# Sigmoid attention and a routed feed-forward block on one core: a third PSUM buffer for the scores, two single banks shared by everything else, and the input loads cut and ordered anew

## The chip, the cores and the metric

The kernel runs on one core of one Trainium2 chip. The metric is the device time of one execution in microseconds (us), lower is better. A core has five engines that run side by side: TensorE (PE in the profile, with its weight loads as PEld), VectorE (DVE), ScalarE (ACT), GpSimd (POOL) and SyncE (SP), which here only issues DMA transfers. PSUM, the memory that TensorE writes its results to, has 8 banks of 512 fp32 columns for each partition.

## What is computed

Everything is fp32. Attention with a sigmoid in place of the softmax runs over 8 sequences, 12 heads, 448 tokens and head size 64. Then, for each sequence, the 128 tokens with the highest gate score pass through a two-layer feed-forward block, and the result is added to their rows.

```python
scores = scale * np.matmul(q, k.transpose(0, 1, 3, 2)) - np.log(S)
attn = 1.0 / (1.0 + np.exp(-scores))
x = np.matmul(attn, v)            # (B,H,S,D) -> (B,S,H*D) = (8,448,768)
scores = np.einsum('bsd,d->bs', x, w_gate)
out = x.copy()
for b in range(B):
    top_idx = np.argpartition(-scores[b], capacity)[:capacity]     # capacity 128
    xe = x[b, top_idx]
    ye = np.maximum(xe @ w1, 0.0) @ w2                             # 768 -> 1024 -> 768
    g = 1.0 / (1.0 + np.exp(-scores[b, top_idx]))
    out[b, top_idx] = x[b, top_idx] + g[:, None] * ye
```

## The kernel before

The attention is cut into 24 **items** of four heads (two pairs), three items to a sequence. The order on every engine is the order in which `stream` writes the program out (L378 to L396).

For item `i`, `load` (L71) brings k, q and the item's part of v, 16 DMAs on SP, two items ahead. The two raw buffers of k and q are free again once `turn` has read them. Every DMA of SP also waits for the one issued eight before it, so at most eight are under way. `turn` (L155) turns k and q over on VectorE, one item ahead. `scores` (L169) makes the scores in seven steps, `n` = 0 to 6: a pair of matmuls into one two-bank PSUM buffer `psc`, then one sigmoid on ScalarE (L185) that reads it into `attnT`. Steps 0 to 2 are the first pair of heads, 3 to 5 the second, 6 the last 64 tokens of both. `psc` has two buffers, so step `n` waits for the sigmoid of step `n - 2`. `values` (L188) multiplies by v into two banks `pav`: first the last 64 tokens (L194, from `raw_h`), then the full blocks (L200, from `raw_v`); VectorE copies each bank out to `xT` (L205).

An item stands in `stream` as: steps 0 to 3, `fill(2i)`, steps 4 to 6, `turn(i+1)`, `fill(2i+1)`, `values(i)`. `fill(s)` (L366) writes what two tables hold for **slot** `s`:

- `back` (L212): slots `2i+2` and `2i+3`. TensorE transposes one pair of heads of item `i` into the single bank `ps1` (L219); VectorE copies it into `x_b` (L221), the sequence's rows. There is one `x_b`.
- `store_and_gate` (L226), `rank` (L244), `select` (L269), `turn_rows` (L288) of sequence `b`, at slots 6b+7, +9, +11 and +12: the rows go out by two 1.3 MB stores on SP (to the output and to a scratch copy `x_d`, L228 and L230), the gate is computed on VectorE, the tokens are ranked (L247 to L265), the chosen rows are gathered by POOL from `x_d` (L283) and transposed. All their PSUM results are in `ps1`.
- `ffn1` (L298) and `ffn2` (L311), slots 6b+13 to 6b+18, in the single bank `psf`: four slots with two of the eight 128-column blocks of the hidden layer each, with a relu on ScalarE after four blocks (L309); then two slots with 384 output columns each, closed by VectorE (L324). `scatter` (L328) writes the rows back to the output. A later sequence's stores wait for it on SP.

So there are 2 x 2 banks for `psc`, 2 for `pav`, 1 for `ps1` and 1 for `psf`: all 8. Slots 48 and up stand behind the last item (the **tail**). `load_weights` (L148) issues both weight matrices (3 MB each) as two DMAs on POOL's queue; in POOL's own order nothing holds them, so they start at the very beginning.

Of the kernel before, what the change touches and what calls it, by code (L numbers as in the profile page):

```python
# [16 lines left out]
def kernel(  # L17
# [51 lines left out]
    raws = {}  # L69

    def load(i):  # L71
        b, g = divmod(i, NQ)
# [1 line left out]
        tiles = []
        for nm, src in (("k", k), ("q", q)):

            t = raw.tile([P, 2, TB * Dh], F32, name=f"raw_{nm}")
            for j in range(2):
                for e in range(2):
                    p0 = (2 * j + e) * TT  # L80
                    nc.sync.dma_start(
                        out=t[p0:p0 + TT, :, 0:RUN],
                        in_=bass.AP(
                            tensor=src.tensor,
                            offset=src.offset + (b * H + h0 + j) * S * Dh + e * TT,
                            ap=[[TB * Dh, TT], [2 * S * Dh, 2], [1, RUN]]),
                    )
            tiles.append(t)

        tv = vals.tile([P, 4, NF * Dh], F32, name="raw_v")  # L90
        for m in range(4):
            nc.sync.dma_start(
                out=tv[m * TT:(m + 1) * TT],
                in_=bass.AP(tensor=v.tensor,
                            offset=v.offset + (b * H + h0) * S * Dh + NF * m * Dh,
                            ap=[[TB * Dh, TT], [S * Dh, 4], [1, NF * Dh]]))

        th = vals.tile([P, 2, Dh], F32, name="raw_h")
        for pr in range(2):
            for m in range(2):  # L100
                p0 = (2 * pr + m) * TT
                nc.sync.dma_start(
                    out=th[p0:p0 + TT],
                    in_=bass.AP(tensor=v.tensor,
                                offset=(v.offset + (b * H + h0 + 2 * pr) * S * Dh
                                        + (4 * NF + m) * Dh),
                                ap=[[TB * Dh, TT], [S * Dh, 2], [1, Dh]]))
# [47 lines left out]
    def turn(i):  # L155
# [3 lines left out]
        src = raws[i][0].rearrange("p a (r d) -> p a r d", d=Dh)
        for pr in range(2):  # L160
            nc.vector.transpose(  # L161
                kT[i][:, pr, :4 * NF],
                src[:, pr, :4 * NF, 0:TT].rearrange("p (m c) d -> p c m d", c=NF))
        nc.vector.transpose(kT[i][:, :, 4 * NF:], src[:, :, 4 * NF:, 0:TT])
        qT[i] = head.tile([P, 2, TB, TT], F32, name="qT")
        src = raws[i][1].rearrange("p a (r d) -> p a r d", d=Dh)
        nc.vector.transpose(qT[i], src[:, :, :, 0:TT])  # L167
# [20 lines left out]
    def values(i):  # L188
        tv, th = raws[i][2:]
        out_t = [ps_o.tile([P, S], F32, name="pav") for _ in range(2)]  # L190
        for pr in range(2):
            for j in range(2):
                p = slice(pr * Dh, (pr + 1) * Dh)
                nc.tensor.matmul(out_t[pr][j * Dh:(j + 1) * Dh], th[p, j, :],  # L194
                                 attn[i][p, 2 * NF, j, :], start=True, stop=False)
        xT[i] = head.tile([P, 2, S], F32, name="xT")
        for pr in range(2):
            for c in range(NF):
                for j in range(2):
                    nc.tensor.matmul(  # L200
                        out_t[pr][j * Dh:(j + 1) * Dh],
                        tv[:, 2 * pr + j, c * Dh:(c + 1) * Dh],
                        attn[i][:, pr * NF + c, j, :],
                        start=False, stop=(c == NF - 1))
            nc.vector.tensor_copy(  # L205
                xT[i][:, pr].rearrange("p (t r) -> p r t", r=TB),
                out_t[pr].rearrange("p (r t) -> p r t", t=TT))
        del raws[i], qT[i], kT[i], attn[i]
# [220 lines left out]
```

## Time and profile before

| | |
|---|---|
| runs | median 584.09 us of 3 (583.95 to 584.29) |
| the profiled execution | 583.43 us, of which the span of the profile is 581.7 us |
| TensorE busy | 514.4 us, 88% of the span |
| VectorE, ScalarE, POOL busy | 235.8 us (41%), 174.0 us (30%), 31.3 us (5%) |
| the 16 DMA engines | 88.93 MB moved; share busy 0.8 to 0.9 in the first quarter of the span, mostly 0.2 to 0.7 in the rest |

"Busy" counts a matmul's record from its start to its modelled end. Matmuls are pipelined, so records overlap, and a stretch can read as busy although TensorE begins nothing in it. What a wait costs is read from the distance between the starts of two instructions instead. Each fp32 matmul has two records, so "x8" in a row of the trace is four matmuls; the listings of the program's order further down count matmuls.

### The profile page before, as it was taken

The numbers are of one execution on the slowest core, as the hardware profiler recorded it, in microseconds if no ns is written. First come the engines' busy times: TensorE is split into PE (matmuls) and PEld (weight loads), VectorE is DVE, ScalarE is ACT, GpSimd is POOL, SyncE is SP. The second block draws the span as 40 slices with busy tenths as digits, with TensorE's granted clock in tenths as the row PEclk, the third lists the DMA queues.
The fourth block names the chain that finished last, engine by engine and source line by source line (L and its number), as shares of the span: only waits on it lengthen the run. The fifth ranks groups of instructions, "written<-read, shape, count | busy, mean of one in ns | idle before, by whom it ended". The sixth has DMA issues, their size and how long they took to land.

```text
span 581.7 us, 7332 instructions
## 1 busy us (share of the span) xinstructions
PE 514.4 (88%) x2896; PEld 271.3 (47%) x2896; DVE 235.8 (41%) x481; ACT 174.0 (30%) x193; POOL 31.3 (5%) x43
## 2 busy tenths in 40 slices
PE   0819996889999999999999999999999999998995
PEld 0203332334554455545554455545544554558582
DVE  0013353635372356426371356326371456137100
ACT  0404444233522332522522422522532422400000
POOL 5000000000000000001000000001000000000100
PEclk9978999898999999999999999999999999999998
DMA  8999999893976188724976198724875150006000
GB/s 199 333 230 205 208 197 274 191 216 107 237 160 149 44 264 194 167 70 149 221 159 147 59 266 191 163 60 169 215 160 132 59 191 1 0 28 219 27 28 27
DMA packets 46995, 88.93 MB, mean 153 GB/s; under 512 B 12848, under 2 KB 25136, under 8 KB 46960
## 3 DMA queue, kind: packets, MB, share of 16 engines
q1 hardware_dynamic: 44288, 75.52, 53.0%
q0 software_dynamic: 2672, 12.93, 7.0%
q8 instruction: 23, 0.38, 0.3%
q14 instruction: 12, 0.10, 0.1%
HBM read 63.26 MB, written 25.17 MB: 152 GB/s over the span
## 4 chain that ended last, share of the span: by engine, by line
PE 71%; DMA 9%; ACT 8%; issue 6%; DVE 4%; SPq 0%; POOLq 0%; POOL 0%; ACTq 0%; DVEq 0%
PE psc L180 19%; PE pav L200 18%; PE psf L320 12%; PE psf L306 11%; ACT attnT L185 8%; DMA raw_q<-in_q_dram 5%; PE ps L219 4%; PE pav L194 4%; DMA raw_h<-in_v_dram 2%; DMA x_d<-x_b 2%; DVE junk L234 1%; PE ps L247 1%; PE ps L274 1%; DVE junk L259 1%; PE ps L294 1%
## 5 line engine op out<-in xcount | busy, mean ns | idle before, releaser
L185 ACT ACTIVATE attnT<-psc,bias_s 128x896 f32<-128x896 f32 x168 | 161.7, 1005 | 287.3 <-PE psc L180 287.2
L180 PE MATMUL psc<-qT,kT 64*128 64x448 f32 (+1 forms) x768 | 160.0, 584 | 46.2 <-DVE qT L167 28.7
L180 PEld LDWEIGHTS psc<-qT,kT 64*128 64x128 f32 (+1 forms) x768 | 54.5, 178 | 137.9 <-ACT attnT L185 70.8
L200 PE MATMUL pav<-attnT,raw_v 128*64 128x448 f32 x576 | 113.7, 544 | 0.0
L306 PE MATMUL psf<-xeT,w_sb 128*128 128x128 f32 x768 | 92.2, 276 | 1.7 <-DVE oe L324 1.0
L320 PE MATMUL psf<-w_sb,hT 128*128 128x384 f32 x256 | 90.8, 497 | 1.9 <-DVE oe L324 1.2
L306 PEld LDWEIGHTS psf<-xeT,w_sb 128*128 128x128 f32 x768 | 88.4, 192 | 2.8 <-DVE oe L324 1.8
L221 DVE COPY x_b<-ps 112x512 f32<-112x512 f32 x48 | 33.1, 689 | 135.1 <-PE ps L219 122.0
L200 PEld LDWEIGHTS pav<-attnT,raw_v 128*64 128x64 f32 x576 | 39.3, 137 | 73.5 <-issue 70.7
L205 DVE COPY xT<-pav 128x448 f32<-128x448 f32 x48 | 43.0, 922 | 52.9 <-PE pav L200 52.9
L320 PEld LDWEIGHTS psf<-w_sb,hT 128*128 128x128 f32 x256 | 46.7, 194 | 28.4 <-DVE oe L324 2.1
L161 DVE STREAM_TRANSPOSE kT<-raw_k 128x384 f32<-128x384 f32 x48 | 24.7, 552 | 29.2 <-DMA raw_k<-in_k_dram 29.2
L219 PEld LDWEIGHTS ps<-iden,xT 128*112 128x112 f32 x192 | 19.8, 134 | 35.6 <-issue 25.8
L219 PE MATMUL ps<-iden,xT 128*112 128x128 f32 x192 | 31.5, 287 | 3.2 <-DVE x_b L221 3.2
L309 ACT ACTIVATE hT<-psf 128x512 f32<-128x512 f32 x16 | 9.6, 597 | 78.5 <-PE psf L306 78.5
L234 DVE CUSTOM_DVE_ANT_0 junk<-x_b,wg_b 112x768 f32<-112x768 f32 x32 | 30.7, 958 | 1.8
L324 DVE SCALAR_TENSOR_TENSOR oe<-psf,gate,xe 128x384 f32<-128x384 f32 x16 | 9.9, 617 | 52.4 <-PE psf L320 30.2
L167 DVE STREAM_TRANSPOSE qT<-raw_q 128x896 f32<-128x896 f32 x24 | 25.8, 1075 | 10.5 <-DMA raw_h<-in_v_dram 6.4
L194 PE MATMUL pav<-attnT,raw_h 64*64 64x448 f32 x192 | 24.9, 578 | 2.8 <-ACT attnT L185 2.8
L259 DVE SCALAR_TENSOR_TENSOR junk<-rep,earlier 112x448 f32<-112x448 f32 x32 | 21.9, 685 | 1.4
L259 DVE SCALAR_TENSOR_TENSOR junk<-rep,ones_row 112x448 f32<-112x448 f32 x32 | 21.9, 685 | 1.2
L283 POOL DMA_INDIRECT xe<-x_d,row x8 | 8.0, 1006 | 266.8 <-DVE idx L279 229.5
(38 smaller groups left out, 117.6 us busy)
## 6 DMA issues: line engine op xcount, KB each, us to landing
raw_k<-in_k_dram SPq DMA_DIRECT2D x96, 216.0 KB, 4.8
raw_q<-in_q_dram SPq DMA_DIRECT2D x96, 216.0 KB, 6.8
out_dram<-x_b SPq DMA_DIRECT2D x8, 1344.0 KB, 6.5
x_d<-x_b SPq DMA_DIRECT2D x8, 1344.0 KB, 11.4
raw_v<-in_v_dram SPq DMA_DIRECT2D x96, 96.0 KB, 4.3
w_sb<-in_moe_w_dram POOLq DMA_DIRECT2D x2, 3072.0 KB, 25.9
raw_h<-in_v_dram SPq DMA_DIRECT2D x96, 16.0 KB, 2.4
wg_b<-in_moe_w_gate_dram POOLq DMA_DIRECT2D x1, 336.0 KB, 8.2
```

The costliest lines, as they stand in the source:

```text
L167: nc.vector.transpose(qT[i], src[:, :, :, 0:TT])
L180: nc.tensor.matmul(psc[p0:p0 + np_, j, :S], kT[i][d, pr, rows, :].rearrange("e r t -> e (r t)"), qT[i][d, pr].rearrange("e r t -> e (r t)" ...
L185: nc.scalar.activation(attn[i][:, n], psc[:, :, :S], AF.Sigmoid, bias=bias_s, scale=QK_SCALE)
L194: nc.tensor.matmul(out_t[pr][j * Dh:(j + 1) * Dh], th[p, j, :], attn[i][p, 2 * NF, j, :], start=True, stop=False)
L200: nc.tensor.matmul(out_t[pr][j * Dh:(j + 1) * Dh], tv[:, 2 * pr + j, c * Dh:(c + 1) * Dh], attn[i][:, pr * NF + c, j, :], start=False, sto ...
L205: nc.vector.tensor_copy(xT[i][:, pr].rearrange("p (t r) -> p r t", r=TB), out_t[pr].rearrange("p (r t) -> p r t", t=TT))
L219: nc.tensor.transpose(ps[:CP, c, :], xT[i][:, pr, c * CP:(c + 1) * CP], iden)
L221: nc.vector.tensor_copy(x_tiles[b][:, :, hp * P:(hp + 1) * P], ps[:CP])
L234: nc.vector.tensor_tensor_reduce(out=junk, in0=x_b[:, c, :], in1=wg_b, scale=1.0, scalar=0.0, op0=ALU.mult, op1=ALU.add, accum_out=tg[:, c ...
L259: nc.vector.scalar_tensor_tensor(out=junk, in0=rep[:, :S], scalar=rep[:, S + c:S + c + 1], in1=mask, op0=cmp, op1=ALU.mult, accum_out=cnt[ ...
L306: nc.tensor.matmul(ps[:, f % 4, :n], w1_sb[:, t, f * P:(f + 1) * P], xeT[:, t, :n], start=(t == 0), stop=(t == KD - 1))
L320: nc.tensor.matmul(ps[:n, :ND], hT[:, t, :n], w2_sb[:, t, cols], start=(t == 0), stop=(t == KF - 1))
```

## The change

Banks: `psc` gets a third two-bank buffer (6 banks). The other two banks are the single buffers `oa` and `ob`. `oa` takes the first half of `values`, `back`, `rank`, `select` and `turn_rows`; `ob` takes the second half of `values`, `ffn1` and `ffn2`.

Order within `values`: the full blocks of the first pair, the last 64 tokens of both, the full blocks of the second pair. Each half is copied out as before.

Feed-forward: `ffn1` takes three slots (blocks 3, 3, 2, a relu after each), `ffn2` three slots with 256 columns each. The six slots stay the same.

Loads: item 0's k and q come by pair (8 + 8 small DMAs), and `turn(0)` works by pair. v comes per sequence, all 12 heads in 8 DMAs, into two buffers; its last 64 tokens are loaded to both halves of the partitions, twice the bytes of before for that part. Sequence 0's v comes in two parts around item 1's load; later ones are issued at item `3b+1`. The weights are cut in 14 pieces on SP, two at each item 1 to 7, behind that item's loads.

```diff
-    ND = D // 2
+    ND = D // 3
-    vals = ctx.enter_context(tc.tile_pool(name="vals", bufs=3))
+    vals = ctx.enter_context(tc.tile_pool(name="vals", bufs=2))
-    ps_sc = ctx.enter_context(tc.tile_pool(name="ps_sc", bufs=2, space=PSUM))
-    ps_o = ctx.enter_context(tc.tile_pool(name="ps_o", bufs=2, space=PSUM))
-    ps_f = ctx.enter_context(tc.tile_pool(name="ps_f", bufs=1, space=PSUM))
-    ps_1 = ctx.enter_context(tc.tile_pool(name="ps_1", bufs=1, space=PSUM))
+    ps_sc = ctx.enter_context(tc.tile_pool(name="ps_sc", bufs=3, space=PSUM))
+    ps_a = ctx.enter_context(tc.tile_pool(name="ps_a", bufs=1, space=PSUM))
+    ps_b = ctx.enter_context(tc.tile_pool(name="ps_b", bufs=1, space=PSUM))
...
+    def load_v(b, h0=0, h1=H):
+        if h0 == 0:
+            raw_v[b] = (vals.tile([P, H, NF * Dh], F32, name="raw_v"),
+                        vals.tile([P, H, Dh], F32, name="raw_h"))
+        tv, th = raw_v[b]
...
+        for m in range(4):
+            nc.sync.dma_start(out=tv[m * TT:(m + 1) * TT, h0:h1], in_=rows(NF * m, NF))
+        for m in range(4):
+            nc.sync.dma_start(out=th[m * TT:(m + 1) * TT, h0:h1],
+                              in_=rows(4 * NF + m % 2, 1))
 
-    load(0)
+    load(0, (slice(0, 1), slice(1, 2)))
+    load_v(0, 0, 4)
     load(1)
+    load_v(0, 4, H)
...
-    def load_weights():
-        for w, src in ((w1_sb, moe_w1), (w2_sb, moe_w2)):
-            nc.gpsimd.dma_start(out=w, in_=src.rearrange("(t p) f -> p t f", p=P))
+    def load_weights(i):
+        for n in (2 * i - 2, 2 * i - 1):
+            if 0 <= n < KD:
+                nc.sync.dma_start(out=w1_sb[:, n], in_=moe_w1[n * P:(n + 1) * P, :])
+            elif KD <= n < KD + KF:
+                n -= KD
+                nc.sync.dma_start(out=w2_sb[:, n], in_=moe_w2[n * P:(n + 1) * P, :])
...
     def values(i):
...
+        out_t = [ps_a.tile([P, 512], F32, name="oa"), ps_b.tile([P, 512], F32, name="ob")]
...
+        full(0, True, False)
         for pr in range(2):
             for j in range(2):
                 p = slice(pr * Dh, (pr + 1) * Dh)
...
+                nc.tensor.matmul(out_t[pr][j * Dh:(j + 1) * Dh, :S],
+                                 th[p, 4 * g + 2 * pr + j, :],
+                                 attn[i][p, 2 * NF, j, :], start=(pr == 1), stop=(pr == 0))
+        out(0)
+        full(1, False, True)
+        out(1)
...
-            for f in range(KF):
-                put(long, s + 2 + f // 2, ffn1, b, n, f)
-            s += 2 + KF // 2
-            for part in range(2):
+            s += 2
+            for f0 in range(0, KF, 3):
+                f1 = min(f0 + 3, KF)
+                for f in range(f0, f1):
+                    put(long, s, ffn1, b, n, f0, f1, f)
+                s += 1
+            for part in range(D // ND):
                 for t0 in range(0, KF, 2):
-                    put(long, s + part, ffn2, b, n, part, t0)
-            put(long, s + 1, scatter, b, n)
-            s += 2
+                    put(long, s, ffn2, b, n, part, t0)
+                s += 1
+            put(long, s - 1, scatter, b, n)
...
-        turn(0)
+        turn(0, (slice(0, 1), slice(1, 2)))
         late_consts()
         for i in range(NI):
             if i + 2 < NI:
                 load(i + 2)
-            if i == 1:
-                load_weights()
+            if i % NQ == 1 and i // NQ + 1 < B:
+                load_v(i // NQ + 1)
+            load_weights(i)
```

Three places show how this moves instructions. The first is SP's queue from the start of the program to the load of item 2. Before (the number behind a tile's name tells its buffers apart):

```order
L81 DMA raw_k_87<-in_k_dram 32x2x864 x4
L81 DMA raw_q_92<-in_q_dram 32x2x864 x4
L92 DMA raw_v_97<-in_v_dram 32x4x192 x4
L102 DMA raw_h_102<-in_v_dram 32x2x64 x4
L81 DMA raw_k_107<-in_k_dram 32x2x864 x4
L81 DMA raw_q_112<-in_q_dram 32x2x864 x4
L92 DMA raw_v_117<-in_v_dram 32x4x192 x4
L102 DMA raw_h_122<-in_v_dram 32x2x64 x4
L81 DMA raw_k_170<-in_k_dram 32x2x864 x4
L81 DMA raw_q_175<-in_q_dram 32x2x864 x4
```

The same queue in the change, up to the first two weight pieces (`raw_k_84` and `raw_q_85` are item 0's):

```order
L82 DMA raw_q_85<-in_q_dram 32x864 x4
L105 DMA raw_v_102<-in_v_dram 32x4x192 x4
L107 DMA raw_h_103<-in_v_dram 32x4x64 x4
L82 DMA raw_k_112<-in_k_dram 32x2x864 x4
L82 DMA raw_q_113<-in_q_dram 32x2x864 x4
L105 DMA raw_v_102<-in_v_dram 32x8x192 x4
L107 DMA raw_h_103<-in_v_dram 32x8x64 x4
L82 DMA raw_k_175<-in_k_dram 32x2x864 x4
...
L105 DMA raw_v_253<-in_v_dram 32x12x192 x4
L107 DMA raw_h_254<-in_v_dram 32x12x64 x4
L154 DMA w1_sb_137<-in_moe_w1_dram 128x1024 x2
```

The load of item 2 (`raw_k_175`) now stands behind the whole of sequence 0's v, and the weights stand in this queue, behind the loads, instead of in POOL's.

The second place is TensorE from the second half of an item, through `values`, to the next item's first half. Before:

```order
L306 MATMUL psf<-xeT,w_sb 128x128 x12
L194 MATMUL pav<-attnT,raw_h 64x448 x4
L200 MATMUL pav<-attnT,raw_v 64x448 x12
L180 MATMUL psc<-qT,kT 128x448 x8
L219 MATMUL ps_2571<-iden,xT 112x128 x4
```

In the change:

```order
L324 MATMUL ob<-xeT,w_sb 128x128 x18
L205 MATMUL oa<-attnT,raw_v 64x448 x6
L220 MATMUL oa<-attnT,raw_h 64x448 x2
L220 MATMUL ob<-attnT,raw_h 64x448 x2
L205 MATMUL ob<-attnT,raw_v 64x448 x6
L188 MATMUL psc<-qT,kT 128x448 x8
L237 MATMUL oa<-iden,xT 112x128 x4
```

The value matmuls now write the banks that the feed-forward block (`ob`) and the transposes of `back` (`oa`) have just used and will use next, and the last 64 tokens stand in their middle.

The third place is TensorE in the tail, from the last `back` on. Before:

```order
L219 MATMUL ps_3200<-iden,xT 112x128 x4
L306 MATMUL psf<-xeT,w_sb 128x128 x24
L247 MATMUL ps_3246<-diag,ones 112x448
L249 MATMUL ps_3246<-tok_gate_142,iden 112x4
L306 MATMUL psf<-xeT,w_sb 128x128 x24
L274 MATMUL ps_3301<-tok_gate_142,sel 128x2 x4
L320 MATMUL psf<-w_sb,hT 128x384 x8
```

In the change:

```order
L237 MATMUL oa<-iden,xT 112x128 x4
L324 MATMUL ob<-xeT,w_sb 128x128 x36
L265 MATMUL oa<-diag,ones 112x448
L267 MATMUL oa<-tok_gate_145,iden 112x4
L324 MATMUL ob<-xeT,w_sb 128x128 x12
L338 MATMUL ob<-w_sb,hT 128x256 x8
L292 MATMUL oa<-tok_gate_145,sel 128x2 x4
```

The last sequence's `rank` (L247, now L265) stands behind 36 matmuls of the sequence before it instead of 24, and its `select` behind one more group of eight.

## Rows read from the trace of the kernel before

**Rows 1.** Timeline of the start: start us, length us, engine, line, what [idle before, releaser].

```profile
44.07 5.81 PE L180 MATMUL psc<-qT,kT 64*128 64x448 f32 x16 [13.09 <-DVE qT L167]
...
74.84 1.77 PE L180 MATMUL psc<-qT,kT 64*128 64x448 f32 x8
...
89.37 1.77 PE L180 MATMUL psc<-qT,kT 64*128 64x448 f32 x8
...
99.59 0.69 DVE L221 COPY x_b<-ps 112x512 f32<-112x512 f32 x1 [9.18 <-DMA x_d<-x_b]
...
139.16 2.84 PE L306 MATMUL psf<-xeT,w_sb 128*128 128x128 f32 x24
```

**Rows 2.** Waits over the whole span: engine line <- releaser: us, times, longest.

```profile
PEld psc L180 <- ACT attnT L185: 70.8, 79, 1.3
...
DVE x_b L221 <- DMA x_d<-x_b: 13.1, 2, 9.2
```

**Rows 3.** Timeline of one item in the middle: TensorE, ScalarE, one copy of VectorE.

```profile
206.95 0.98 PE L194 MATMUL pav<-attnT,raw_h 64*64 64x448 f32 x8
207.86 4.73 PE L200 MATMUL pav<-attnT,raw_v 128*64 128x448 f32 x24
212.52 1.77 PE L180 MATMUL psc<-qT,kT 64*128 64x448 f32 x8
213.65 1.91 ACT L185 ACTIVATE attnT<-psc,bias_s 128x896 f32<-128x896 f32 x2 [8.82 <-PE psc L180]
214.71 1.92 PE L180 MATMUL psc<-qT,kT 64*128 64x448 f32 x8 [0.42 <-ACT attnT L185]
216.56 0.65 PE L219 MATMUL ps<-iden,xT 128*112 128x128 f32 x4
...
217.25 0.69 DVE L221 COPY x_b<-ps 112x512 f32<-112x512 f32 x1 [3.69 <-PE ps L219]
...
219.82 1.77 PE L180 MATMUL psc<-qT,kT 64*128 64x448 f32 x8
221.95 0.98 PE L180 MATMUL psc<-qT,kT 64*64 64x448 f32 x8 [0.35 <-ACT attnT L185]
222.87 0.65 PE L219 MATMUL ps<-iden,xT 128*112 128x128 f32 x4
```

**Rows 4.** Page part 6, DMA issues: how many, KB each, median us to landing.

```profile
raw_k<-in_k_dram SPq DMA_DIRECT2D x96, 216.0 KB, 4.8
...
x_d<-x_b SPq DMA_DIRECT2D x8, 1344.0 KB, 11.4
raw_v<-in_v_dram SPq DMA_DIRECT2D x96, 96.0 KB, 4.3
w_sb<-in_moe_w_dram POOLq DMA_DIRECT2D x2, 3072.0 KB, 25.9
raw_h<-in_v_dram SPq DMA_DIRECT2D x96, 16.0 KB, 2.4
```

**Rows 5.** Windows: last three columns are PEclk, DMA share, GB/s.

```profile
2.00:14.00 12.00, 0.00 (x0) 0.00 (x0) 1.23 (x3) 0.24 (x1) 6.70 (x14) 1.00 1.00 223
14.00:38.00 24.00, 13.74 (x64) 4.64 (x64) 2.34 (x4) 6.76 (x7) 0.00 (x0) 0.95 1.03 314
```

**Rows 6.** Windows of 1 us around TensorE's first long stop; same columns.

```profile
36.00:37.00 1.00, 0.00 (x0) 0.00 (x0) 0.39 (x2) 0.00 (x0) 0.00 (x0) 0.50 1.07 301
...
49.00:50.00 1.00, 1.00 (x6) 0.27 (x5) 0.00 (x0) 1.00 (x2) 0.00 (x0) 0.91 1.05 211
```

**Rows 7.** Timeline of the tail, TensorE.

```profile
515.27 0.65 PE L219 MATMUL ps<-iden,xT 128*112 128x128 f32 x4
...
544.33 0.49 PE L294 MATMUL ps<-iden,xe 128*128 128x128 f32 x3
...
558.10 5.62 PE L306 MATMUL psf<-xeT,w_sb 128*128 128x128 f32 x48 [0.75 <-ACT hT L309]
...
570.61 5.43 PE L320 MATMUL psf<-w_sb,hT 128*128 128x384 f32 x16 [0.77 <-DVE oe L324]
```

More of the change, by code (lines that the diff above doesn't have):

```diff
@@ L72, in load @@
+    ps_b = ctx.enter_context(tc.tile_pool(name="ps_b", bufs=1, space=PSUM))
+    raws, raw_v = {}, {}
+    def load(i, prs=(slice(0, 2),)):
         b, g = divmod(i, NQ)
         h0 = 4 * g
[L74 to L78, printed above, removed]
+        raws[i] = [raw.tile([P, 2, TB * Dh], F32, name=f"raw_{nm}") for nm in "kq"]
+        for pr in prs:
+            for t, src in zip(raws[i], (k, q)):
@@ L79, in load @@
                 for e in range(2):
[L80 to L90, printed above, removed]
@@ L91, in load @@
-        for m in range(4):
[L92 to L107, printed above, removed]
@@ L108, in load @@
-        raws[i] = tiles + [tv, th]
-    load(0)
+                    for j in range(2):
+                        p0 = (2 * j + e) * TT
+                        nc.sync.dma_start(
+                            out=t[p0:p0 + TT, pr, 0:RUN],
+                            in_=bass.AP(
+                                tensor=src.tensor,
+                                offset=(src.offset + e * TT
+                                        + (b * H + h0 + j + 2 * pr.start) * S * Dh),
+                                ap=[[TB * Dh, TT], [2 * S * Dh, pr.stop - pr.start],
+                                    [1, RUN]]))
@@ L146, in late_consts, with turn @@
                 fill=1.0, base=-c * CP, pattern=[[1, S]], channel_multiplier=-1)
[L148 to L150 removed]
+    def load_weights(i):
[5 more added lines that the diff above has]
+                nc.sync.dma_start(out=w2_sb[:, n], in_=moe_w2[n * P:(n + 1) * P, :])
     qT, kT, attn, pav, xT = {}, {}, {}, {}, {}
[L155 removed]
+    def turn(i, prs=(slice(0, 2),)):
         kT[i] = head.tile([P, 2, TB, TT], F32, name="kT")
[L159 to L164, printed above, removed]
[L165 to L167 removed]
+        qT[i] = head.tile([P, 2, TB, TT], F32, name="qT")
+        sk, sq = [t.rearrange("p a (r d) -> p a r d", d=Dh) for t in raws[i]]
+        for a in prs:
+            for pr in range(a.start, a.stop):
+                nc.vector.transpose(
+                    kT[i][:, pr, :4 * NF],
+                    sk[:, pr, :4 * NF, 0:TT].rearrange("p (m c) d -> p c m d", c=NF))
+            nc.vector.transpose(qT[i][:, a], sq[:, a, :, 0:TT])
+            nc.vector.transpose(kT[i][:, a, 4 * NF:], sk[:, a, 4 * NF:, 0:TT])
+        del raws[i]
     def scores(i, n):
@@ L188, in values, with full, out @@
     def values(i):
-        tv, th = raws[i][2:]
-        out_t = [ps_o.tile([P, S], F32, name="pav") for _ in range(2)]
+        b, g = divmod(i, NQ)
+        tv, th = raw_v[b]
+        out_t = [ps_a.tile([P, 512], F32, name="oa"), ps_b.tile([P, 512], F32, name="ob")]
+        xT[i] = head.tile([P, 2, S], F32, name="xT")
+        def full(pr, start, stop):
+            for c in range(NF):
+                for j in range(2):
+                    nc.tensor.matmul(
+                        out_t[pr][j * Dh:(j + 1) * Dh, :S],
+                        tv[:, 4 * g + 2 * pr + j, c * Dh:(c + 1) * Dh],
+                        attn[i][:, pr * NF + c, j, :],
+                        start=start and c == 0, stop=stop and c == NF - 1)
+        def out(pr):
+            nc.vector.tensor_copy(
+                xT[i][:, pr].rearrange("p (t r) -> p r t", r=TB),
+                out_t[pr][:, :S].rearrange("p (r t) -> p r t", t=TT))
+        full(0, True, False)
         for pr in range(2):
@@ L193, in values @@
                 p = slice(pr * Dh, (pr + 1) * Dh)
[L194 to L208, printed above, removed]
+                nc.tensor.matmul(out_t[pr][j * Dh:(j + 1) * Dh, :S],
[4 more added lines that the diff above has]
+        out(1)
+        del qT[i], kT[i], attn[i]
     x_tiles = {}
```

32 lines of the change are left out of this document (17 added, 15 removed).

## The prediction

> **What bounds the kernel now.** I read the page first: TensorE is busy for 88% of the span, no other engine for more than 41%. That does not say that only fewer matmuls can help, because a record that overlaps the next one hides a late start. So I went to the waits [rows 2]: TensorE's weight loads for the scores wait 70.8 us for sigmoids, in 79 waits of at most 1.3 us. Then to the timeline of one item in the middle of the run [rows 3], which shows what such a wait costs, and to the start and the tail [rows 1, 7], where TensorE really stands still. The kernel has three parts. In the **start**, up to 139.2 us [rows 1], the DMA queues are full and TensorE waits for them. In the **middle**, up to 515.3 us, TensorE sets the pace. In the **tail**, the last 66.4 us [rows 7], a chain through ranking, gather and the last feed-forward block does.
>
> **The middle: the third score buffer.** Steps 0 to 3 take from 212.52 to 216.56, 4.04 us [rows 3]. The first sigmoid starts 1.13 us in; step 2 waits for it and starts at 214.71, 2.19 us in; step 3 waits for the second. With three buffers steps 0 to 2 need nobody, and step 3 waits for the first sigmoid: it starts 2.19 us in. A last step lasts 0.92 us until what follows it starts (221.95 to 222.87). So what follows starts after 3.11 us, 0.93 us sooner. Steps 4 to 6 take 3.05 us (219.82 to 222.87), because step 6 waits for the sigmoid of step 4. With three buffers none waits: a pair of matmuls takes 0.78 us (six in 207.86 to 212.52), so 2 x 0.78 + 0.92 = 2.48 us, 0.57 us less. The sigmoids then finish later than the scores, but `values` begins with blocks 0 to 2, so that lies beside other work. Gain: 1.50 us an item.
>
> What is added: `values` has its last 64 tokens in the middle, one more change between tile shapes. The tails take 0.91 us (206.95 to 207.86) where a pair takes 0.78, so a change is about 0.15 us. `ffn2` has 24 matmuls of 256 columns for 16 of 384, the same columns; I take 0.1 us a sequence.
>
> **The shared banks** add waits, all on copies by VectorE or ScalarE. `values` now waits for the last copy out of `oa` (`back`, the ranks, or the chosen tokens), a copy that starts 0.7 us after the first of its matmuls (216.56 to 217.25) and lasts up to 0.7 us [rows 3]; between them stand 18 `ffn1` matmuls (4 us), 6 after `rank` (1.3 us), or 4 of `ffn2` (1.7 us), so it is hidden once the feed-forward block runs. The relu or the last copy out of `ob` has the 2.3 us of the first value blocks. The copies of `values` have steps 0 to 3, 3.1 us; only after `rank`, whose long chain on VectorE stands ahead of them, does this come close to the need. I cost all of it at nothing. Without cover a handoff costs what the tail shows, 0.75 us [rows 7]. `x_b` must be stored before the next sequence's first `back`: the trace has two such waits of eight [rows 2], and that interval grows by 6 `ffn1` matmuls (1.3 us) and shrinks by 0.9, so none is added. SP's queue loses its waits for v; nothing new stands ahead of these stores.
>
> From the first feed-forward matmul (139.16) to 515.27 there are 17 first and 17 second halves and 18 `values`: 17 x 1.50 = 25.5 us less, 18 x 0.15 = 2.7 and 6 x 0.1 = 0.6 more. At slot 48 two thirds instead of half of an `ffn2` are done, 1.7 us more ahead of the tail. Net **-20.5 us**.
>
> **The start.** Item 4's first `back` waits for `x_b`'s stores; the second lands at 99.5 us [rows 1], and the first feed-forward matmul follows 39.7 us later. So the landing counts. In SP's queue ahead of it stand six loads of k and q, and v. A load is 8 x 216 KB = 1.77 MB (q's DMAs are as large as k's, [rows 4]), 7.9 us at the 223 GB/s of the first 12 full microseconds [rows 5]; v adds 0.46 MB, 2.1 us. The weights, 6.29 MB at the 314 GB/s seen while they ran, are 20 us; the store landed 11.4 us after its issue [rows 4]. Before: 6 x 10.0 + 20 + 11.4 = 91.4, so 8.1 us are the queue's start, the gate vector and gaps. After: 6 x 7.9 for the loads, 2 x 7.1 for two sequences of v (1.57 MB with the tails doubled), 3 x 3.3 for six of the 14 weight pieces, 11.4: 82.9 us. With the same 8.1 us it lands at 91.0; with only 3.5 us for start and gate vector (an estimate: 2 us until data flows, and 0.34 MB), at 86.4. The new queue has eight large loads under way where the old one had small tails among them, so I take the middle, 88.4.
>
> Is TensorE there by then? Item 1's load lands near 22 us and turning it takes 2.2, so item 1 starts near 24 instead of 44.07. Item 2's load, now behind all of sequence 0's v, lands near 35. Its transposes stand on VectorE ahead of a copy out of `oa`, for which `values(1)` now waits. TensorE stands for about 8 us, and such a stop halves its clock: PEclk is 0.50, the 1.2 GHz level, at 36 us after the stop of 13.09 us and is back to the full one only at 49, 5 us after work resumed [rows 1, 6], 2.6 us lost. Item 2 then starts near 47. An item without a feed-forward block takes 14.5 us now (74.84 to 89.37, [rows 1]) and then about 13.4, so item 4 starts near 74 and its copy is due near 78, before the landing.
>
> Then 39.7 us follow, less 2 x 1.50 for items 5 and 6, plus about 1.1 for uncovered copies before `values` in items 4 and 5: 37.8. First feed-forward matmul at 126.2: **-13.0 us**.
>
> **The tail.** The last `back` comes 1.7 us sooner (one third of an `ffn2` ahead of it, not half). `rank` stands behind 36 `ffn1` matmuls instead of 24: 12 x 0.22 and a handoff, 3.5 us, of which some 2 were waiting for the gate anyway, so the gather starts 1.5 us later; `ffn2` behind it is 1.7 us shorter. So the last `ffn1` starts as far behind 515.27 as now. It then has three groups and three parts instead of two and two: two more handoffs of about 0.75 us with the pipe's drain, less a shorter last copy. **+1.2 us**.
>
> **Sum.** 13.0 + 20.5 - 1.2 = 32.3 us off the profiled execution's 583.43 us gives 551.1; the median of the runs stands 0.66 us above that execution: **552 us**.
>
> One price is missing: v's last 64 tokens are rows of 256 bytes. The Trainium skill (DMA: Bandwidth & Descriptors, Specifications) asks for at least 512 bytes a piece for full rate. At half rate, an estimate, the two sequences' tails (0.79 MB) would land the store 3.5 us later: 555 us. No row prices a tail apart from its queue.
>
> **The rivals.**
> 1. The queue serves no better than now (doubled tails, gaps behind the big v transfers) and the store lands near 101 us: the start gains nothing, 565 us. For: 8.1 us of the queue's time before are unexplained. Against: 10 us of weights leave the way.
> 2. The queue runs without gaps and TensorE keeps its clock: landing near 80, 8 to 10 us more: 543 us.
> 3. The third buffer does not do what it says: a sigmoid step is 0.96 us (two in 1.91) against 0.78 on TensorE, and if ScalarE is late wherever a buffer is wanted, the 25.5 us are gone: 577 us. Against: seven steps are 6.7 us of ScalarE in an item of 13 us or more.
> 4. **Slower.** A handoff on the two single banks is exposed everywhere: two by `back`, two by `values`, in 17.5 items, 70 in all at the tail's 0.75 us, 52 us: 604 us. It decides from 32.3 / 70 = 0.46 us on. The Trainium skill (Perfetto Trace Analysis, Optimizing Tensor Performance) has the rule for this: independent matmul groups should rotate through banks so that emptying one overlaps the next. The tail's bank, reused at once, agrees with 0.75 us. Against: in the middle each bank has 1.3 to 4 us of other matmuls between uses.
>
> **Chances and range.** Forecast, 545 to 560: 0.50. Rival 2: 0.20. Rival 1: 0.15. Rival 3 or some tenths per handoff: 0.10. Rival 4: 0.05. The range 537 to 567 takes in the forecast, rivals 1 and 2 and both ends for the landing. A measurement of this kernel tells 0.2%, 1.2 us, from no change: faster 0.94, same 0.01, slower 0.05.
>
> **What would show it.** Right: weight loads of the scores waiting about a third of 70.8 us; three items in the middle in about 61 us; `x_d` landed between 86 and 91 us and the first feed-forward matmul near 126; the stop of item 1 at `values`, not at the scores; a tail of 67 to 68 us. Wrong: `values` or `back` waiting for a copy in the middle, more than two waits for `x_d`, or the first feed-forward matmul after 135.

## The result, and the profile after

| | before | the changed kernel |
|---|---|---|
| median of the runs (us) | 584.02 (581.84 to 584.29, 4 runs) | 551.69 (547.81 to 553.46, 4 runs) |
| ratio to before | | 0.9445, 95% interval 0.939 to 0.950 |
| profiled execution, its span | 583.43, 581.7 | 551.51, 549.7 |
| start: to the first feed-forward matmul | 139.2 | 124.9 |
| middle: from there to the end of the last item | 376.1 | 360.3 |
| tail: from there to the end of the span | 66.4 | 64.5 |

The forecast was 552.0 us in a range of 537 to 567. The sum is right, but its three terms are not: 13.0 + 20.5 - 1.2 was forecast, 14.3 + 15.8 + 1.9 came. Of the runs further down, one execution with two score buffers (578.69 us) and one with the weights on GpSimd's queue (2880.65 us) were slow for a reason that is not known, and are left out.

The waits over the whole span, as in [rows 2] (engine line <- releaser: us, times, longest):

```profile
PEld psc L188 <- ACT attnT L193: 13.4, 30, 0.7
...
PE oa L205 <- DVE x_b L239: 9.3, 3, 7.7
...
DVE x_b L239 <- DMA x_d<-x_b: 9.3, 1, 9.3
```

The weight loads of the scores wait for sigmoids 13.4 us instead of 70.8, and no longer than 0.7 at a time. In their place stands a wait of `values` for a copy out of `oa`: three times, all ahead of 70 us, once for 7.7 us. One copy waits for the stores of `x_d`, not two.

The timeline of the start, TensorE and VectorE, which answers to [rows 1]:

```profile
24.05 3.28 PE L188 MATMUL psc<-qT,kT 64*128 64x448 f32 x16 [1.50 <-DVE qT L173]
...
36.86 1.11 DVE L173 STREAM_TRANSPOSE qT<-raw_q 128x896 f32<-128x896 f32 x1 [3.93 <-DMA raw_q<-in_q_dram]
...
38.09 0.65 DVE L239 COPY x_b<-oa 112x512 f32<-112x512 f32 x1
...
38.79 4.75 PE L205 MATMUL oa<-attnT,raw_v 128*64 128x448 f32 x12 [7.69 <-DVE x_b L239]
...
47.01 3.28 PE L188 MATMUL psc<-qT,kT 64*128 64x448 f32 x16
...
74.13 3.28 PE L188 MATMUL psc<-qT,kT 64*128 64x448 f32 x16
...
84.49 0.69 DVE L239 COPY x_b<-oa 112x512 f32<-112x512 f32 x1 [9.32 <-DMA x_d<-x_b]
...
124.90 4.18 PE L324 MATMUL ob<-xeT,w_sb 128*128 128x128 f32 x36
```

Item 1 starts at 24.05 instead of 44.07. Then TensorE stops for 7.69 us ahead of `values(1)`: the copy out of `oa` that it needs (38.09) stands on VectorE behind the transposes of item 2, and these wait for item 2's q. The copy of item 4 waits until 84.49 for the store. The clock at the two stops (windows; the last three columns are PEclk, the granted clock of TensorE as a share of full speed, the DMA share and GB/s):

```profile
34.00:44.00 10.00, 5.21 (x16) 1.54 (x20) 1.88 (x3) 0.00 (x0) 0.00 (x0) 0.50 1.05 227
44.00:46.00 2.00, 2.00 (x16) 0.63 (x10) 0.93 (x1) 0.00 (x0) 0.00 (x0) 1.00 1.14 202
...
86.00:94.00 8.00, 5.59 (x16) 2.28 (x16) 5.42 (x14) 0.00 (x0) 0.00 (x0) 0.50 1.10 215
```

PEclk is 0.50, the 1.2 GHz level, from 34 to 44 us, though TensorE works again from 38.79, and once more from 86 to 94, behind the wait for the store. Windows of 1 us show a third fall, to 0.50 from 109 to 112.

An item in the middle, TensorE, as in [rows 3]:

```profile
196.84 3.28 PE L188 MATMUL psc<-qT,kT 64*128 64x448 f32 x16
200.05 0.65 PE L237 MATMUL oa<-iden,xT 128*112 128x128 f32 x4
...
204.65 2.69 PE L188 MATMUL psc<-qT,kT 64*128 64x448 f32 x16
207.26 0.65 PE L237 MATMUL oa<-iden,xT 128*112 128x128 f32 x4
```

Steps 0 to 3 take 3.21 us (196.84 to 200.05) instead of 4.04, steps 4 to 6 take 2.61 instead of 3.05: 1.27 us an item. Each is now one run of matmuls without a gap, and steps 0 to 3 take 0.80 us a step.

The tail, TensorE and POOL, as in [rows 7]:

```profile
485.19 0.65 PE L237 MATMUL oa<-iden,xT 128*112 128x128 f32 x4
...
509.37 3.72 PE L338 MATMUL ob<-w_sb,hT 128*128 128x256 f32 x16
...
509.91 1.00 POOL L301 DMA_INDIRECT xe<-x_d,row  x1 [12.88 <-DVE idx L297]
...
513.90 0.52 PE L312 MATMUL oa<-iden,xe 128*128 128x128 f32 x3 [0.81 <-DMA xe<-x_d,row]
...
518.78 4.29 PE L324 MATMUL ob<-xeT,w_sb 128*128 128x128 f32 x36 [0.58 <-DVE oe L342]
523.71 4.29 PE L324 MATMUL ob<-xeT,w_sb 128*128 128x128 f32 x36 [0.64 <-ACT hT L327]
```

The gather is issued 24.7 us behind the last item's end, and its rows are used 4.0 us later. Each of the six groups of the last block waits 0.5 to 0.6 us for the relu or the sum that reads `ob`.

### The profile page after: what moved, and what is told of

Its sections match the earlier page's. It is cut to its first block, busy times and chain, and to the rows that moved or that the text cites. A ratio compares the mean times of both kernels' runs of the same rounds, so it can differ in the third digit from the quotient of the medians.

```text
span 549.7 us, 7413 instructions
## 1 busy us (share of the span) xinstructions
PE 508.6 (93%) x3024; PEld 294.5 (54%) x3024; DVE 238.3 (43%) x491; ACT 169.9 (31%) x201; POOL 29.5 (5%) x41
## 4 chain that ended last, share of the span: by engine, by line
PE 73%; DMA 16%; issue 6%; SPq 3%; DVE 1%; POOLq 0%; ACT 0%; ACTq 0%
PE psc L188 20%; PE ob L338 12%; PE ob L324 12%; PE oa L205 9%; PE ob L205 9%; DMA raw_q<-in_q_dram 5%; PE oa L237 4%; PE oa L220 3%; DMA w_sb<-in_moe_w_dram 3%; DMA raw_k<-in_k_dram 3%; DMA x_d<-x_b 2%; DMA raw_v<-in_v_dram 1%; PE oa L312 1%; PE oa L265 1%; DMA out_dram<-oe,idx 1%
## 5 line engine op out<-in xcount | busy, mean ns | idle before, releaser
L324 PE MATMUL ob<-xeT,w_sb 128*128 128x128 f32 x768 | 91.7, 276 | 2.6 <-ACT hT L327 1.9
L338 PE MATMUL ob<-w_sb,hT 128*128 128x256 f32 x384 | 91.1, 382 | 2.6 <-DVE oe L342 1.2
L324 PEld LDWEIGHTS ob<-xeT,w_sb 128*128 128x128 f32 x768 | 88.1, 192 | 3.8 <-ACT hT L327 2.4
L239 DVE COPY x_b<-oa 112x512 f32<-112x512 f32 x48 | 33.1, 689 | 101.4 <-PE oa L237 92.1
L338 PEld LDWEIGHTS ob<-w_sb,hT 128*128 128x128 f32 x384 | 69.6, 190 | 11.7 <-DVE oe L342 2.0
L205 PE MATMUL oa<-attnT,raw_v 128*64 128x448 f32 x288 | 65.5, 594 | 10.6 <-DVE x_b L239 9.3
L205 PE MATMUL ob<-attnT,raw_v 128*64 128x448 f32 x288 | 59.4, 548 | 0.0
L237 PE MATMUL oa<-iden,xT 128*112 128x128 f32 x192 | 31.6, 288 | 4.6 <-DVE x_b L239 4.6
L173 DVE STREAM_TRANSPOSE qT<-raw_q 128x896 f32<-128x896 f32 (+1 forms) x25 | 26.0, 1039 | 8.4 <-DMA raw_q<-in_q_dram 8.4
L220 PE MATMUL oa<-attnT,raw_h 64*64 64x448 f32 x96 | 23.5, 567 | 0.0
## 6 DMA issues: line engine op xcount, KB each, us to landing
x_d<-x_b SPq DMA_DIRECT2D x8, 1344.0 KB, 11.4
```

Of the source, the lines that this page charges most:

```text
L173: nc.vector.transpose(qT[i][:, a], sq[:, a, :, 0:TT])
L205: nc.tensor.matmul(out_t[pr][j * Dh:(j + 1) * Dh, :S], tv[:, 4 * g + 2 * pr + j, c * Dh:(c + 1) * Dh], attn[i][:, pr * NF + c, j, :], star ...
L220: nc.tensor.matmul(out_t[pr][j * Dh:(j + 1) * Dh, :S], th[p, 4 * g + 2 * pr + j, :], attn[i][p, 2 * NF, j, :], start=(pr == 1), stop=(pr = ...
L237: nc.tensor.transpose(ps[:CP, c, :], xT[i][:, pr, c * CP:(c + 1) * CP], iden)
L239: nc.vector.tensor_copy(x_tiles[b][:, :, hp * P:(hp + 1) * P], ps[:CP])
L324: nc.tensor.matmul(ps[:, f - f0, :n], w1_sb[:, t, f * P:(f + 1) * P], xeT[:, t, :n], start=(t == 0), stop=(t == KD - 1))
```

## The experiments

All runs by stage, in us, of the profiled execution of each: the start of the first feed-forward matmul, from there to the end of the last item (where the transposes of `back` behind the last `values` start), from there to the end of the span.

| | median of the runs | start | middle | tail |
|---|---|---|---|---|
| before | 584.02 | 139.2 | 376.1 | 66.4 |
| the change | 551.69 | 124.9 | 360.3 | 64.5 |
| two score buffers | 575.96 (3 runs) | 127.9 | 381.8 | 64.6 |
| two of each bank | 560.80 | 120.3 | 381.1 | 57.5 |
| weights on GpSimd's queue | 561.5 to 563.3 (3 runs) | 134.8 | 360.3 | 64.7 |
| two buffers for `x_b` | 541.98 | 114.7 | 360.3 | 64.6 |
| loads alone | 570.33 | 126.3 | 376.1 | 66.3 |
| banks alone | 567.51 | 140.2 | 360.3 | 64.8 |
| tail in score buffers | 544.81 | 127.8 | 360.3 | 57.9 |
| tails of v not doubled | 555.22 | 129.1 | 360.3 | 64.7 |
| `x_b` and item 2's transposes | 543.77 | 116.0 | 360.3 | 64.5 |
| all three edits | 536.62 | 112.4 | 360.3 | 57.9 |
| six items' transposes | 531.44 | 111.5 | 360.3 | 57.9 |

The middle is the same to 0.1 us wherever its instructions are the same. The start is not: the change and the run "tail in score buffers" have the same program there, and their starts take 124.9 and 127.8; the four executions of the change spread over 5.7 us. So a single start says something from some 6 us on.

### The third buffer, and the single banks

```diff
-    ps_sc = ... bufs=3
+    ps_sc = ... bufs=2
```

> The changed kernel with two score buffers again instead of three; two PSUM banks stay idle. Theory (the third buffer is worth about 1.27 us an item, 18 items, and nothing else gives that): 574 us (572 to 577), the score weight loads wait for sigmoids some 60 to 70 us again, and the first feed-forward matmul still starts near 125. Rival 3 (the sigmoids set the pace anyway, the loads are all of the gain): 553 us or less.

And, with that edit:

```diff
-    ps_a = ... bufs=1
-    ps_b = ... bufs=1
+    ps_a = ... bufs=2
+    ps_b = ... bufs=2
```

> As the run with two score buffers, but the two shared banks are doubled (2 + 2 + 2 buffers), so that no copy out of one stands ahead of the next use. Theory (the single banks are hidden in the middle, and cost some 0.6 us a handoff only at the start and in the tail, 8 to 10 handoffs): 4 to 7 us below the run with two score buffers, nearly all of it outside of the middle. Rival 4 (handoffs on the single banks are exposed everywhere): 15 us or more below it, most of it in the middle.

With two score buffers: 576.0 us (568.1 to 576.2), ratio to before 0.980 (0.971 to 0.989), so whether it is 2% faster stays unclear. With two of each: 560.8, ratio 0.958 (0.953 to 0.964). The period of a sequence is read from the chain of waits (start us, us, what), first two score buffers:

```profile
193.97 4.02 PE ob L324 x36
...
259.61 4.02 PE ob L324 x36
```

then two of each,

```profile
186.28 4.02 PE ob L324 x36
...
251.78 4.02 PE ob L324 x36
```

the change,

```profile
187.17 4.02 PE ob L324 x36
...
249.03 4.02 PE ob L324 x36
```

and the kernel before:

```profile
204.34 2.68 PE psf L306 x24
...
269.35 2.68 PE psf L306 x24
```

A period is 65.64 and 65.50 us; in the change it is 61.86, before it was 65.01. So the third buffer gives 3.78 us a sequence (65.64 - 61.86), 1.26 an item, and rival 3 falls. What the change adds beside it costs 0.63 a sequence (65.64 - 65.01): 0.49 is left with two of each bank (65.50 - 65.01), which is then the new order of `values` and the smaller parts (0.55 was forecast), and 0.14 is the single banks. Rival 4 falls in the middle. This was measured with two score buffers; with three no bank is left to double, and there the trace alone speaks: it lists no wait of TensorE's matmuls from 124.9 to 485 us. But over the whole run the single banks cost 15.3 us (574.2 and 558.9, the two spans), where the theory had 4 to 7: 7.6 at the start, 0.7 in the middle and 7.1 in the tail. Neither side had it whole: the size is rival 4's, the place is the theory's. At the start the stop ahead of `values(1)` is gone with two of each, but the store still lands at 84.3 us, as with single banks (84.4); what is gained lies behind the landing, 36.1 us to the first feed-forward matmul for 43.5. This is the last block with two of each, TensorE:

```profile
532.25 10.88 PE L324 MATMUL ob<-xeT,w_sb 128*128 128x128 f32 x96
542.96 10.53 PE L338 MATMUL ob<-w_sb,hT 128*128 128x256 f32 x48
```

All 48 + 24 matmuls of the last block run without a stop.

### Where the weights stand

```diff
-                nc.sync.dma_start(out=w1_sb[:, n], in_=moe_w1[n * P:(n + 1) * P, :])
...
+        if i != 1:
+            return
+        for w, src in ((w1_sb, moe_w1), (w2_sb, moe_w2)):
+            nc.gpsimd.dma_start(out=w, in_=src.rearrange("(t p) f -> p t f", p=P))
```

> The changed kernel with the weights as in the kernel before: two whole DMAs on GpSimd's queue at item 1, instead of 14 pieces behind the loads on SyncE's. Theory (6.29 MB of weights then stand beside the loads ahead of x_b's store, of which 2.9 MB were there already; 3.5 MB more at 314 GB/s is 11 us): first feed-forward matmul 8 to 12 us later than 124.9, 561 us (558 to 564). Rival (where the weights stand does not matter, because the queues share the bandwidth and the store waits its turn either way): 552 us.

Ratio 0.964 (0.960 to 0.969), the first feed-forward matmul at 134.8: 9.9 us later than in the change, as the theory has it. Only the start moves.

### The store of `x_d`

```diff
-            x_tiles[b] = moe.tile([CP, NCH, D], F32, name="x_b")
+            x_tiles[b] = moe.tile([CP, NCH, D], F32, name="x_b", bufs=2)
...
-                junk = moe.tile([CP, S], F32, name="junk2")
+                junk = moe.tile([CP, D], F32, name="junk")
...
```

> The changed kernel with two buffers for x_b (two scratch tiles of the ranking share one, to make room), so that item 4's first back does not wait for the stores of sequence 0. Theory (that wait, 9.3 us at 84.5, is what the start ends on): 542 to 544 us, first feed-forward matmul near 116. Rival (a later load or the weights are the next thing to wait for and take back more than half): 547 us or more.

541.98 us, ratio 0.929 (0.926 to 0.933): 9.7 below the change. The start on TensorE:

```profile
81.23 0.98 PE L265 MATMUL oa<-diag,ones 112*112 112x448 f32 x2 [0.88 <-DVE x_b L239]
...
114.74 4.18 PE L324 MATMUL ob<-xeT,w_sb 128*128 128x128 f32 x36
```

The wait for the store was what the start ended on, and nothing of its size took its place.

### Loads alone, banks alone

The kernel before with the change's `load`, `load_v`, `load_weights` and `turn`:

```diff
-    vals = ctx.enter_context(tc.tile_pool(name="vals", bufs=3))
+    vals = ctx.enter_context(tc.tile_pool(name="vals", bufs=2))
...
+            if i % NQ == 1 and i // NQ + 1 < B:
+                load_v(i // NQ + 1)
+            load_weights(i)
```

> The kernel before with the loads of the changed one alone (v by sequence, q and k of the first item by pair, weights in pieces on SyncE); banks and feed-forward blocks as before. Theory (start and middle are gained apart from each other): x_d of sequence 0 lands near 84 instead of 99.5, first feed-forward matmul 15 us earlier, near 124; period of a sequence 65.0 and tail 66 as before: 568 us (566 to 571). Rival (the loads gain only together with the third buffer, since TensorE is late anyway): 575 us or more.

And the change with these of the kernel before:

```diff
-            load_weights(i)
+            if i == 1:
+                load_weights()
```

> The changed kernel with the loads of the kernel before: only the banks and the shape of the feed-forward blocks are new. Theory: the store lands near 99.5 as before and decides the start (first feed-forward matmul 139 to 141), the period of a sequence is 61.9 and the tail 64.5 as in the changed kernel: 566.5 us (564 to 569). Rival (a shorter item also brings the start forward): 560 us or less.

570.3 us, ratio 0.974 (0.968 to 0.980), and 567.5, ratio 0.972 (0.969 to 0.975). The loads move the start alone (12.8 us), the banks the middle and the tail alone (15.8 and 1.6; the start 1.0 later). Their sum is 29.2, the change's 32.0; the rest lies in the start, within what single starts differ by. So the two halves of the change are gained apart from each other, as both theories had it.

### The tail without the single bank

```diff
+    tail = []
+    def ffn_bank():
+        if tail:
+            return ps_sc.tile([P, 2, 512], F32, name="psc")[:, 0]
+        return ps_b.tile([P, 512], F32, name="ob")
...
-            st[b]["ob"] = ps_b.tile(...)
+            st[b]["ob"] = ffn_bank()
...
+        tail.append(True)
```

The list `tail` is filled behind the last `values`.

> The changed kernel, but behind the last item the feed-forward blocks take their banks from the three score buffers, which are idle by then, in place of the one shared bank. Theory (the tail's stops between groups are the single bank's; with two banks of each it was 7.1 us shorter): the tail from the last item's end 6 us shorter (5 to 7), nothing else moves: 546 us. Rival (the stops are the wait for relu and for the gated sum, whose results the next group needs): 551 us or more.

544.8 us, ratio 0.932 (0.928 to 0.936). The tail is 6.6 us shorter:

```profile
519.39 10.88 PE L331 MATMUL psc<-xeT,w_sb 128*128 128x128 f32 x96
530.11 10.52 PE L345 MATMUL psc<-w_sb,hT 128*128 128x256 f32 x48
```

No stop of 0.5 to 0.6 us is left between the groups. So the stops were the bank's, not the wait for relu's result.

### The tails of v

```diff
-            nc.sync.dma_start(out=th[m * TT:(m + 1) * TT, h0:h1], in_=rows(4 * NF + m % 2, 1))
+            for h in range(h0 + 2 * (m // 2), h1, 4):
+                nc.sync.dma_start(out=th[m * TT:(m + 1) * TT, h:h + 2], ...
```

> The changed kernel, but each 64 token tail of v is loaded for the heads that read it alone: 0.39 MB less in a sequence, in more and smaller DMAs (12 in a sequence, not 4). Rows of 256 bytes at full rate: 0.39 MB in each of two sequences ahead of the first store are worth 0.79 MB / 236 GB/s = 3.3 us, landing near 81 instead of 84.4, 548 us. At half rate (the Trainium skill, DMA: Bandwidth & Descriptors, Specifications; an estimate): 6.7 us, landing near 78, 545 us. Rival (what counts is SyncE's issue time, 0.46 us for a DMA: 12 more issues ahead of the store eat 5.5 us): 552 us or more.

The expectation counts the bytes twice: a sequence loads 0.20 MB (12 DMAs of 16 KB) for 0.39 (4 of 96 KB), so the two sequences are worth 1.7 us at the full rate and 3.3 at half. It came to 555.2 us, ratio 0.950 (0.946 to 0.954): not faster, as the rival has it; the store lands at 87.3 us for 84.4, and the start takes 129.1. SyncE's issues in the change (start us, us, what):

```profile
41.48 5.06 SPq L107 DMA_DIRECT2D raw_h<-in_v_dram  x4
```

and with the smaller DMAs:

```profile
41.00 10.24 SPq L108 DMA_DIRECT2D raw_h<-in_v_dram  x12
```

The windows of these stretches (DMA share and GB/s are the last two columns), first the change:

```profile
23.00:41.00 18.00, 9.26 (x46) 4.06 (x48) 6.29 (x10) 6.51 (x7) 0.00 (x0) 0.80 1.08 227
42.00:50.00 8.00, 8.00 (x42) 2.59 (x38) 1.85 (x2) 1.86 (x3) 0.00 (x0) 0.88 1.21 200
```

then the smaller DMAs:

```profile
41.00:51.00 10.00, 10.00 (x52) 3.80 (x50) 2.56 (x4) 3.47 (x4) 0.00 (x0) 0.92 0.79 145
```

Half the bytes took twice the time, 0.85 us for each DMA, and the DMA engines were not full meanwhile (share 0.79). SyncE's waits from 41.0 to 51.3 us say why (engine line <- releaser: us, times, longest):

```profile
SPq L108 <- DMA raw_v<-in_v_dram: 3.9, 4, 1.2
SPq L108 <- DMA raw_q<-in_q_dram: 2.1, 4, 0.6
```

An issue itself takes 0.31 us (the median of the 12). 6.0 of the 10.2 us are eight waits for the landing of the transfer issued eight before, four of q and four of v: the program's limit of eight transfers under way, which the small ones fill as the large ones did. The time that the rival expects is lost there, but more of it in waits than in issues.

In the change the DMA engines are full while the tails pass (1.21), at 200 GB/s for the 227 of the 18 us ahead: 27 GB/s for 8 us are 0.22 MB, 0.9 us at 227. So the trace leaves room for a price of 0.9 us for the rows of 256 bytes, but no run takes them apart from the k and the weights that flow beside them, and the change's landing came 4 us sooner than forecast. The Trainium skill (DMA: Bandwidth & Descriptors, Specifications) asks for at least 512 bytes for the full rate; half rate for the 0.39 MB, an estimate, would be 1.7 us, about twice the 0.9 of the trace.

### A version that beats both

All three have two buffers for `x_b`. The first puts the transposes of item 2 behind the copy that `values(1)` needs, the second adds the tail's edit, the third does so with the transposes of the first six items.

```diff
-            if i + 1 < NI:
+            if i + 1 < NI and i != 1:          # third: i >= 2 * NQ
                 turn(i + 1)
             fill(2 * i + 1)
+            if i == 1:                         # third: i < 2 * NQ
+                turn(i + 1)
```

> The changed kernel with two buffers for x_b and, in item 1, the transposes of item 2 behind the second back of item 0 on VectorE, so that the values of item 1 need not wait for item 2's load. Theory (the stop of 7.4 us at 38 is VectorE's order, not the load itself: q of item 2 is there at 36, and values of item 1, 7 us, fit ahead of it): item 2 starts at 38 to 39 instead of 46.2, TensorE keeps its full clock, 534 to 536 us. Rival (the load of item 3, or the weights, is late next): 538.5 us or more.

> The changed kernel with three edits: two buffers for x_b, the transposes of item 2 behind the second back of item 0 on VectorE, and the score buffers for the feed-forward blocks of the tail. Theory (start, middle and tail add up: 9.7 us from x_b, 6 to 7.5 from the transposes, 6.6 from the tail, off 551.7): 528 to 530 us, span from the last item's end 58, first feed-forward matmul near 108. Rival (the DMA queue is the next wait and takes back the transposes' gain): 535 us or more.

> As the run with all three edits, but the transposes of the next item stand behind the second back in each of the first six items, not in item 1 alone. Theory (in the run with all three edits the stop only moved: item 4's load lands at 62.4, its transposes hold the copy that values of item 3 need, TensorE stops for 5.4 us and loses its full clock; with values of item 3 ahead of them item 4 starts near 65 instead of 72.4, and then item 5's load, landing near 85, is the next): 531 to 534 us. Rival (the queue decides whatever the order, the first feed-forward matmul stays at 112 or comes later): 536 us or more.

The first: 543.8 us, ratio 0.933 (0.928 to 0.937), no gain over `x_b` alone. Its start, TensorE and VectorE:

```profile
38.05 3.28 PE L188 MATMUL psc<-qT,kT 64*128 64x448 f32 x16
...
62.72 1.11 DVE L173 STREAM_TRANSPOSE qT<-raw_q 128x896 f32<-128x896 f32 x1 [2.46 <-DMA raw_q<-in_q_dram]
...
64.66 4.59 PE L205 MATMUL oa<-attnT,raw_v 128*64 128x448 f32 x12 [5.80 <-DVE x_b L239]
```

Item 2 starts at 38.05 instead of 46.18, as the theory has it, but the stop only moves, to `values(3)` behind item 4's transposes. The rival, a later load (item 4's), holds. The second: 536.6 us, ratio 0.920 (0.917 to 0.924), of which the tail gives 6.6; the same stop is there, and the rival's time (535 or more) came. The third: 531.4 us (531.0 to 533.9), ratio 0.913 (0.910 to 0.916), inside the theory's 531 to 534:

```profile
64.86 3.28 PE L188 MATMUL psc<-qT,kT 64*128 64x448 f32 x16
...
83.82 4.97 PE L188 MATMUL psc<-qT,kT 64*128 64x448 f32 x16 [3.44 <-DVE qT L173]
...
111.52 4.18 PE L331 MATMUL ob<-xeT,w_sb 128*128 128x128 f32 x36
```

Item 4 starts at 64.86 instead of 72.38 in the second. What stops item 5 for 3.44 us is not its load, as I had expected, but the ranking's chain ahead of its transposes on VectorE:

```profile
80.95 0.87 DVE L283 TENSOR_SCALAR sel<-iota_r,above 112x128 f32<-112x128 f32 x4
81.74 1.03 DVE L170 STREAM_TRANSPOSE kT<-raw_k 128x384 f32<-128x384 f32 x2
```

The transposes follow it without a wait for a DMA. In this one profiled start the gain over the second is only 0.9 us (111.5 and 112.4), in the medians 5.2: the second's runs spread from 532.4 to 539.0, and its profiled one is the shortest. The spread goes with the granted clock: that shortest run has a mean of 0.993, the longest 0.981. The first and the second are the same program up to the tail, both stop at `values(3)`, and their profiled starts differ by 3.5 us (116.0 and 112.4): from 80 to 86 and from 98 to 104 us PEclk is 0.72 in the first and 1.00 in the second. Why the clock fell there in one and not in the other is open.

## Why the prediction was right, and where its terms were not

- **The third buffer**: the mechanism holds (step 3 is the first to wait, its weight load starts at 199.03, 2.19 us in as forecast, and in the middle nothing is late behind it), the size is 1.27 us an item for the forecast 1.50. The steps that failed are "3.11 us" and "2.48 us", put together from pieces of 0.78, 0.92 and 2.19: the steps run back to back at 0.80, which makes 3.21 and 2.61. 17 x 1.27 = 21.6 instead of 25.5 is 3.9 of the 4.7 us that the middle fell short. The additions (2.7 + 0.6 and the 1.7 of the earlier `ffn2`, 5.0 in all) measured 5.0 (381.1 - 376.1, with two of each bank).
- **The single banks in the middle**: costed at nothing, they cost 0.14 us a sequence, 0.7 in all, most of what is left of the 4.7. No `values` and no `back` waits for a copy there.
- **The start**: the order of events came as forecast: item 1 near 24 (24.05), the stop ahead of `values(1)` of about 8 us (7.69), the half clock, item 2 near 47 (47.01), item 4 near 74 (74.13). The landing was forecast at 88.4 (the middle of 86.4 and 91.0 would be 88.7), from an issue near 77 and 11.4 us to land; SyncE came to the store at 71.08, close to the 71.5 that its terms give without "the queue's start, the gate vector and gaps", and it landed 13.3 us later, at 84.4. The other way, 40.5 us instead of 37.8 follow the landing. The step that failed there is "Then 39.7 us follow, less 2 x 1.50": items 5 and 6 gave 2.5 us, not 3.0, the uncovered copies took 1.4 for 1.1, and the remaining 1.9 are nearly all TensorE's clock, which the step took over as it was. The kernel before loses its full clock twice behind the landing too (windows, the third column from the end is PEclk):

```profile
100.00:105.00 5.00, 2.96 (x8) 1.70 (x8) 2.99 (x6) 0.00 (x0) 0.00 (x0) 0.54 1.03 219
...
135.00:136.00 1.00, 1.00 (x4) 0.35 (x2) 1.00 (x4) 0.00 (x0) 0.00 (x0) 0.50 0.00 0
```

In the change the low clock falls on other work, from 85 to 95 us and from 109 to 112: `values` of items 4 and 5 take 7.9 and 7.4 us for 6.6 and 5.6, 3.1 more. In the kernel before its second stretch, from 135 to 138, falls on steps 4 to 6 of item 6, which take 4.3 us for 2.6 in the change, 1.2 more than the third buffer explains. The shorter landing and the longer way together: 14.3 for 13.0.
- **The tail**: forecast 1.2 us longer, it is 1.9 shorter. The last block is 1.0 longer for the forecast 1.2 (30.9 from 518.78 to the end, 30.0 before). The step that failed is "so the last `ffn1` starts as far behind 515.27 as now". It let the 6.2 us from the gather's issue to the transposes at 544.33 [rows 7] stand as the gather's own in both kernels. Two rows (TensorE, POOL) and a window of the kernel before, which the forecast did not use, show another limit:

```profile
537.51 6.98 PE L320 MATMUL psf<-w_sb,hT 128*128 128x384 f32 x16
...
538.12 1.00 POOL L283 DMA_INDIRECT xe<-x_d,row  x1 [9.93 <-DVE idx L279]
```

```profile
536.00:542.00 6.00, 5.48 (x17) 3.61 (x18) 1.15 (x7) 0.17 (x1) 1.00 (x1) 0.72 0.25 71
```

The part of `ffn2` ahead of those transposes took 6.98 us at a granted clock of 0.72 in the mean; the same 16 records take 5.43 in the last block [rows 7]. No DMA moves anything from 542 to 552 us, so the rows were there before 544.33: TensorE was late there, not the gather. In the change this part is a third of `ffn2` and at full clock (3.72), and the gather decides, after 4.0 us: 2.2 us less, where the forecast had none. The work behind it is 2.5 us shorter for the forecast 1.7 (4.9 us from 513.90 to 518.78, 7.4 from 544.33 to 551.73 before), the gather 1.9 later for the forecast 1.5. The four, 1.9 - 2.2 - 2.5 + 1.0, make up the tail to 0.1 us.
- **The rivals**: 1 (the queue no better) and 2 (landing near 80) bracket the landing of 84.4, which lies nearer to 2. Rival 3 fell by the run with two score buffers, rival 4 by the run with two of each for the middle; at the two ends its handoffs cost 14.7 us (7.6 and 7.1). The rule of the Trainium skill that rival 4 names (Perfetto Trace Analysis, Optimizing Tensor Performance), that matmul groups rotate through banks, agrees with the runs at the two ends and is worth next to nothing in the middle. Of the 14.7 us the forecast held 1.1 us of copies and two handoffs of the tail; the stop at `values(1)`, which it held too, is not among them, because the landing hides it.
- **The signs**: the stop of item 1 at `values`, three items in 61.86 us and the first feed-forward matmul at 124.9 came as listed. The waits for sigmoids (13.4 us, a fifth of 70.8 and not a third), the landing (84.4, ahead of 86 to 91) and the tail (64.5, not 67 to 68) did not; of the signs of being wrong none came.
- So the terms were off by +1.3, -4.7 and +3.1 us, and the sum by 0.3 only because they cancel. That is luck; what the runs bear out is the sign and the place of the two gains, at the start and in the middle.

## What to carry to other kernels

A single buffer costs next to nothing where other work of its engine stands between two uses (0.14 us a sequence here), and its full handoff wherever the program thins out (14.7 us at the two ends): price it apart at start, middle and tail, and in the tail use the buffers that have gone idle. In a start that waits for loads, look at what stands behind the waiting instruction in its own queue: a transpose that waits for the next load held up a copy that the present work needed. Before calling a gap a transfer's latency, look at what the engines and the granted clock do in it.
